# Grouped-query decode attention on one core: 8 MB tiles in three buffers, keys transposed in place, scores kept in PSUM

## The chip, the cores and the metric

The kernel runs on one core of a Trainium2 chip. The metric is device time in microseconds (us) of one execution. A core has TensorE (PE, matrix products; PEld is its weight load), VectorE (DVE), ScalarE (ACT), GpSimd (POOL) and SyncE (SP), each with its own queue of instructions, and 16 DMA engines. SP and ScalarE each have a queue of their own for the DMAs that they issue. SBUF is the on-chip memory of 128 partitions; PSUM is where TensorE writes.

## The reference

One query token attends to 65536 keys; 32 query heads share 8 heads of keys and values (4 query heads for each group), with head size 128, all in bf16.

```python
B, Hq, Hkv, Sq, Sk, D = 1, 32, 8, 1, 65536, 128
rep = Hq // Hkv
k = jnp.repeat(k, rep, axis=1)
v = jnp.repeat(v, rep, axis=1)
scores = jnp.einsum("bhqd,bhkd->bhqk", q, k) * D ** -0.5
p = softmax(scores, axis=-1)
out = jnp.einsum("bhqk,bhkd->bhqd", p, v)
```

Keys and values are 134 MB each, and every byte is needed once.

## The kernel before

The 65536 keys of a group lie as 512 rows on each of 128 partitions. A group's keys come as four tiles `kn` of 128 rows a partition (32 KB a partition, 4 MB), its values as four tiles `vb` of the same shape. All of them pass through one pool, `iopool`, with four buffers, and SP issues every load (L121 for keys, L202 for values). A load waits on SP until its buffer is free, and all later loads wait behind it.

The outer loop runs over groups g = 0..8, the inner one over tiles s = 0..3. In each turn `k_step(g, s)` works on a key tile of group g and `v_stream(g - 1, s)` on a value tile of the group before, so loads alternate key, value, key, value after the first four key tiles. The order of loads on SP is that of the program; a scheduler merges the instructions of the compute engines.

`k_step`: VectorE transposes 32x32 blocks of the key tile as 32-bit words (L135), two of eight row groups `w` at a time, from `kn` into a tile `T` (pool `tpool`, three buffers). TensorE multiplies with weights `wq` that hold the four queries at shifted columns (L144): 32 matmuls of 512 columns for a tile, all summed in one PSUM tile `sc` of 128x512. ScalarE copies `sc` to SBUF, into `S_g` (L151). There are two weight tiles, `Wq[0]` and `Wq[1]`, which GpSimd fills in turn (`queries`, L109).

`softmax(g)`: VectorE takes the maximum of `S_g` over 2048 columns (L156), TensorE and VectorE spread it over partitions (L160 to L174), ScalarE takes the exp of all 2048 columns into `E_g` with row sums (L177), and VectorE transposes `E_g` into `ET` (`transpose_weights`, L190). `E_g` and `ET` have two buffers each.

`v_stream`: 32 matmuls for a tile (L213), with 32 columns of `ET` as weights and 512 columns of values:

```python
for c in range(rows // W):
    for x in range(2):
        j = 2 * x + c % 2
        nc.tensor.matmul(out=o_tiles[g][32 * j:32 * j + 32, :, :], ...)
```

So j, the group of 32 output rows, runs 0, 2, 1, 3. `pick(g)` keeps the wanted blocks of `psum_o` (L224, L230), `finish` sums them, divides by the row sums and stores. The last value tile comes in pieces of 64, 32, 16, 8, 4 and 4 rows, and `finish_last` works them off with a written-out order on TensorE (L290, L287, L280, L297) up to the last store (L305).

At the start ScalarE issues four small loads of the queries, `qn` (L70), while SP issues the first key tiles. VectorE transposes `qn` and fills `wq` from it before the first keys can be used.

Of the kernel before, what the change touches and what calls it, by code (L numbers as in the profile page):

```python
# [13 lines left out]
NT = 128  # L14
NW = 16
# [5 lines left out]
def kernel(  # L21
# [26 lines left out]
    W = NT // NW  # L48
    assert W * HPG == 32 and KT == 4
# [6 lines left out]
    iopool = ctx.enter_context(tc.tile_pool(name="iopool", bufs=4))  # L56
    tpool = ctx.enter_context(tc.tile_pool(name="tpool", bufs=3))
    spool = ctx.enter_context(tc.tile_pool(name="spool", bufs=2))
    epool = ctx.enter_context(tc.tile_pool(name="epool", bufs=2))
    opool = ctx.enter_context(tc.tile_pool(name="opool", bufs=2))  # L60
    stats = ctx.enter_context(tc.tile_pool(name="stats", bufs=2))
    psc = ctx.enter_context(tc.tile_pool(name="psc", bufs=3, space=bass.MemoryType.PSUM))
    psm = ctx.enter_context(tc.tile_pool(name="psm", bufs=1, space=bass.MemoryType.PSUM))
    psf = ctx.enter_context(tc.tile_pool(name="psf", bufs=1, space=bass.MemoryType.PSUM))
# [3 lines left out]
    qn = const.tile([P, D], bf16)  # L68
    for a in range(4):
        nc.scalar.dma_start(out=qn[32 * a:32 * a + 32, :], in_=q[0, :, 0, :])  # L70
# [3 lines left out]
    Wq = []  # L74
    for x in range(2):
        wq = const.tile([P, 4 * WX], bf16, name=f"wq{x}")
        nc.vector.memset(wq[:, :], 0.0)
        Wq.append(wq)
# [17 lines left out]
    lsum_all = const.tile([P, Hkv], fp32)  # L96
    o_all = const.tile([P, Hkv, D], fp32)

# [5 lines left out]
    def queries(g):  # L104
        eng = nc.vector if g == 0 else nc.gpsimd
        wv = Wq[g % 2][:, :].rearrange("p (b r x) -> p b r x", b=2, r=2)
        for a in range(4):
            qd = slice(32 * a, 32 * a + 32)
            eng.tensor_copy(  # L109
                out=wv[qd, :, :, 32 * a + 28:32 * a + 28 + HPG],  # L110
                in_=qv[qd, :, :, g * HPG:(g + 1) * HPG],
            )
# [3 lines left out]
    S_tiles, E_tiles, ET_tiles, o_tiles = {}, {}, {}, {}  # L116

    def k_load(g, s):
        kn = iopool.tile([P, NT, D], bf16, name="kn", tag="io", align_bytes=2048)
        src = k[0, g].rearrange("(p n) d -> p n d", p=P)  # L120
        nc.sync.dma_start(out=kn[:, :, :], in_=src[:, s * NT:(s + 1) * NT, :])  # L121
        return kn

    def k_step(g, s, kn):
        if s == 0:
            S_tiles[g] = spool.tile([P, KT, 4 * P], fp32, name="S_g")
        wq = Wq[g % 2]
        kv = kn[:, :, :].rearrange("p (c w) d -> p w c d", w=W)
        sc = psc.tile([P, 4 * P], fp32, name="sc")
        for w in range(W):  # L130
            if s == 0 and w == W // 2 and g > 0:
                transpose_weights(g - 1)
            if w % 2 == 0:
                T = tpool.tile([P, 2, NW, D], bf16, name="T")
                nc.vector.transpose(  # L135
                    out=T[:, :, :, :].bitcast(fp32),
                    in_=kv[:, w:w + 2].bitcast(fp32),
                )
            Tv = T[:, w % 2].rearrange("p n (b i r) -> p n b i r", b=2, r=2)
            for b in range(2):  # L140
                for r in range(2):
                    bp = 2 * b + r
                    at = bp * WX + 28 - 4 * w
                    nc.tensor.matmul(  # L144
                        out=sc[:, :],
                        lhsT=wq[:, at:at + P],
                        rhs=Tv[:, :, b, :, r],
                        start=(w == 0 and bp == 0),
                        stop=(w == W - 1 and bp == 3),
                    )  # L150
        nc.scalar.copy(out=S_tiles[g][:, s, :], in_=sc[:, :])  # L151

    def softmax(g):
        S_g = S_tiles[g]
        mx = stats.tile([P, 1], fp32, name="mx")
        nc.vector.tensor_reduce(  # L156
            out=mx[:, :], in_=S_g[:, :, :].rearrange("p n c -> p (n c)"), axis=AX.X, op=ALU.max
        )
# [6 lines left out]
        mrow = stats.tile([1, P], fp32, name="mrow")  # L165
# [10 lines left out]
        E_g = epool.tile([P, KT, 4 * P], bf16, name="E_g")  # L176
        nc.scalar.activation(  # L177
            out=E_g[:, :, :].rearrange("p s x -> p (s x)"),
            in_=S_g[:, :, :].rearrange("p s x -> p (s x)"),
            func=ACT.Exp,  # L180
            bias=nmb[:, 0:1],
            scale=SCALE,
            accum_out=lsum_all[:, g:g + 1],
        )
        E_tiles[g] = E_g

    def transpose_weights(g):

        ET = epool.tile([P, KT, NW, 32], bf16, name="ET")
        nc.vector.transpose(  # L190
            out=ET[:, :, :, :].rearrange("p s c x -> p (s c x)"),
            in_=E_tiles[g][:, :, :].rearrange("p s x -> p (s x)"),
        )
        ET_tiles[g] = ET

    def v_load(g, s, pieces=(NT,)):
        vb = iopool.tile([P, NT, D], bf16, name="vb", tag="io", align_bytes=2048)
        src = v[0, g].rearrange("(p n) d -> p n d", p=P)
        x = 0
        for step in pieces:  # L200
            n0 = s * NT + x
            nc.sync.dma_start(out=vb[:, x:x + step, :], in_=src[:, n0:n0 + step, :])  # L202
            x += step
        return vb

    def v_stream(g, s, vb, rows, last):

        if s == 0:
            o_tiles[g] = pso.tile([P, 4, D], fp32, name="psum_o")
        for c in range(rows // W):  # L210
            for x in range(2):
                j = 2 * x + c % 2
                nc.tensor.matmul(  # L213
                    out=o_tiles[g][32 * j:32 * j + 32, :, :],
                    lhsT=ET_tiles[g][:, s, c, :],
                    rhs=vb[:, c * W + 4 * x:c * W + 4 * x + 4, :],
                    start=(s == 0 and c < 2),
                    stop=(last and c >= rows // W - 2),
                )

    def pick(g):

        o_m = opool.tile([P, 4, D], fp32, name="o_m")
        nc.vector.tensor_tensor(  # L224
            out=o_m[:, :, :],
            in0=o_tiles[g][:, :, :],
            in1=mask[:, :].unsqueeze(2).broadcast_to([P, 4, D]),
            op=ALU.mult,
        )
        nc.vector.tensor_reduce(  # L230
            out=o_all[:, g, :], in_=o_m[:, :, :].rearrange("p x d -> p d x"), axis=AX.X, op=ALU.add
        )

    def sums(g0, n):

        psum_l = psm.tile([HPG, n], fp32, name="psum_l", tag="misc")
        nc.tensor.matmul(out=psum_l[:, :], lhsT=sel[:, :], rhs=lsum_all[:, g0:g0 + n], start=True, stop=True)  # L237
        rl = stats.tile([HPG, n], fp32, name="rl")
        nc.vector.reciprocal(out=rl[:, :], in_=psum_l[:, :])
        return rl  # L240

    def store(g0, n, psum_f, rl):
        o_out = stats.tile([HPG, n, D], bf16, name="o_out")
        nc.vector.tensor_tensor(  # L244
            out=o_out[:, :, :],
# [5 lines left out]
            out=out[0, :, 0, :].rearrange("(g h) d -> h g d", h=HPG)[:, g0:g0 + n, :], in_=o_out[:, :, :]  # L251
        )

    def finish(g0, n):
        rl = sums(g0, n)
        psum_f = psf.tile([HPG, n, D], fp32, name="psum_f", tag="fin")
        nc.tensor.matmul(  # L257
            out=psum_f[:, :, :], lhsT=sel[:, :], rhs=o_all[:, g0:g0 + n, :], start=True, stop=True
        )
        store(g0, n, psum_f, rl)  # L260

    def finish_last(g, s, vb):
# [6 lines left out]
        v_stream(g, s, vb, n1, True)  # L269
        pick(g)  # L270
        psum_oT = pso.tile([P, HPG], fp32, name="psum_oT", tag="psum_o")
        psum_f = psf.tile([HPG, 1, D], fp32, name="psum_f", tag="fin")

        def w4(n):
            c, w = divmod(n, W)
            return ET[:, s, c, HPG * w:HPG * w + HPG]

        def single(a, b):
            for n in range(a, b):
                nc.tensor.matmul(  # L280
                    out=psum_f[:, 0, :], lhsT=w4(n), rhs=vb[:, n, :], start=False, stop=(n == NT - 1)
                )

        with tc.manual_schedule(engines={mybir.EngineType.PE}):
            for n in range(n1, n2):
                if n == n1 + 32:
                    nc.tensor.matmul(  # L287
                        out=psum_f[:, 0, :], lhsT=sel[:, :], rhs=o_all[:, g, :], start=True, stop=False
                    )
                nc.tensor.matmul(  # L290
                    out=psum_oT[:, :], lhsT=vb[:, n, :], rhs=w4(n), start=(n == n1), stop=(n == n2 - 1)
# [4 lines left out]
            psum_t2 = psm.tile([HPG, D], fp32, name="psum_t2", tag="misc")  # L296
            nc.tensor.transpose(out=psum_t2[:, :], in_=oT[:, :], identity=ident[:, :])  # L297
            single(n3, NT)
        o_t = stats.tile([HPG, D], fp32, name="o_t")
        nc.vector.tensor_scalar_mul(out=o_t[:, :], in0=psum_t2[:, :], scalar1=rl[:, 0:1])  # L300
        o_last = stats.tile([HPG, D], bf16, name="o_last")
        nc.vector.scalar_tensor_tensor(  # L302
            out=o_last[:, :], in0=psum_f[:, 0, :], scalar=rl[:, 0:1], in1=o_t[:, :], op0=ALU.mult, op1=ALU.add
        )
        nc.scalar.dma_start(out=out[0, g * HPG:(g + 1) * HPG, 0, :], in_=o_last[:, :])  # L305

    for g in range(Hkv + 1):
        if 0 < g < Hkv:
            queries(g)
        for s in range(KT):  # L310
            if g < Hkv:
                k_step(g, s, k_load(g, s))
            elif s == 0:
# [45 lines left out]
```

## Time and profile before

| | |
|---|---|
| median of 3 runs | 631.85 us (631.57 to 631.9) |
| profiled execution, its own time | 631.69 us |
| its span, first to last instruction | 629.6 us |
| granted TensorE clock, mean | 0.780 |
| TensorE busy | 363.2 us (58%), 2133 instructions |
| VectorE busy | 340.4 us (54%), 201 instructions |
| ScalarE busy | 36.8 us (6%) |
| GpSimd busy | 6.4 us (1%) |
| HBM read | 268.47 MB, 426 GB/s over the span |
| key transposes, L135 | 128 of 2277 ns |
| key matmuls, L144 | 1024, 445 ns |
| value matmuls, L213 | 1008, 403 ns |

Busy times are sums over the span, and the matmuls' means hold the time that they overlap each other. In the profile's slices the span is cut into 40 equal parts (15.7 us here); digits are tenths. A line of a timeline gives start, length, engine, line, operation, output and inputs, count, and in brackets the idle time before it and what ended that. Lines named Lnn are those of the kernel before.

### The profile page before, as it was taken

The numbers are of one execution on the slowest core, as the hardware profiler recorded it, in microseconds if no ns is written. First come the engines' busy times: TensorE is split into PE (matmuls) and PEld (weight loads), VectorE is DVE, ScalarE is ACT, GpSimd is POOL, SyncE is SP. The second block draws the span as 40 slices with busy tenths as digits, with TensorE's granted clock in tenths as the row PEclk, the third lists the DMA queues.
The fourth block names the chain that finished last, engine by engine and source line by source line (L and its number), as shares of the span: only waits on it lengthen the run. The fifth ranks groups of instructions, "written<-read, shape, count | busy, mean of one in ns | idle before, by whom it ended". The sixth has DMA issues, their size and how long they took to land.

```text
span 629.6 us, 4872 instructions
## 1 busy us (share of the span) xinstructions
PE 363.2 (58%) x2133; PEld 141.5 (22%) x2133; DVE 340.4 (54%) x201; ACT 36.8 (6%) x49; POOL 6.4 (1%) x37
## 2 busy tenths in 40 slices
PE   0686836745557554575645856447665466644645
PEld 0232312211222221222211222112221122211212
DVE  0998833774337753377543775436754366553511
ACT  0000100010000100001000010001000010000100
POOL 0000000000000000000000000000000000000000
PEclk9998988767887677876778867788677787767856
DMA  8999999999999999999999999999999999999996
GB/s 369 433 434 431 433 432 434 432 433 433 432 433 432 433 433 432 433 432 433 432 433 433 430 434 434 433 432 433 435 432 433 432 433 433 432 433 434 431 430 267
DMA packets 10192, 268.78 MB, mean 427 GB/s; under 512 B 1340, under 2 KB 1596, under 8 KB 1852
## 3 DMA queue, kind: packets, MB, share of 16 engines
q1 hardware_dynamic: 9936, 268.44, 99.0%
q8 instruction: 16, 0.26, 0.1%
q10 hardware_dynamic: 236, 0.04, 0.0%
q14 instruction: 4, 0.03, 0.0%
HBM read 268.47 MB, written 0.01 MB: 426 GB/s over the span
## 4 chain that ended last, share of the span: by engine, by line
DMA 73%; DVE 12%; issue 11%; PE 2%; ACTq 0%; DVEq 0%; SPq 0%
DMA kn<-in_k_dram 66%; DVE T L135 12%; DMA vb<-in_v_dram 5%; DMA qn<-in_q_dram 2%; PE sc L144 2%; PE psum_o L213 0%; PE psum_oT L290 0%; ACTq L70 0%; PE psum_f L280 0%; DVEq L135 0%; DVE wq L109 0%; PE psum_f L287 0%; DVE sel L83 0%; DVE o_last L302 0%; SPq L202 0%
## 5 line engine op out<-in xcount | busy, mean ns | idle before, releaser
L144 PE MATMUL sc<-T,wq 128*128 128x512 bf16 x1024 | 287.9, 445 | 220.2 <-DVE T L135 220.2
L135 DVE STREAM_TRANSPOSE T<-kn 128x2048 f32<-128x2048 f32 x128 | 284.2, 2277 | 198.6 <-DMA kn<-in_k_dram 198.6
L144 PEld LDWEIGHTS <-wq 128*128 128x128 bf16 x1024 | 109.5, 109 | 394.6 <-issue 159.5
L213 PE MATMUL psum_o<-vb,ET 128*32 128x512 bf16 x1008 | 65.1, 403 | 12.0 <-DMA vb<-in_v_dram 9.8
L151 ACT COPY S_g<-sc 128x512 f32<-128x512 f32 x32 | 18.8, 587 | 510.8 <-PE sc L144 510.8
L213 PEld LDWEIGHTS <-ET 128*32 128x32 bf16 x1008 | 25.5, 100 | 49.2 <-issue 28.3
L156 DVE TENSOR_REDUCE mx<-S_g 128x1 f32<-128x2048 f32 x8 | 18.3, 2286 | 26.1 <-ACT S_g L151 26.1
L190 DVE STREAM_TRANSPOSE ET<-E_g 128x2048 bf16<-128x2048 bf16 x8 | 18.5, 2311 | 16.3 <-ACT E_g L177 16.3
L177 ACT ACTIVATE E_g<-S_g,nmb 128x2048 bf16<-128x2048 f32 x8 | 16.0, 2001 | 47.6 <-DVE nmb L174 40.4
L224 DVE TENSOR_TENSOR o_m<-psum_o,mask 128x512 f32<-128x512 f32 x8 | 5.5, 682 | 21.5 <-PE psum_o L213 21.5
L109 POOL COPY wq<-qx 32x16 bf16<-32x16 bf16 x28 | 5.3, 190 | 426.9 <-PE sc L144 410.2
L160 PE MATMUL psum_t<-ident,mx 128*1 128x128 f32 x8 | 2.2, 270 | 11.2 <-DVE mx L156 11.2
L100 DVE STREAM_TRANSPOSE qx<-qn 128x64 f32<-128x64 f32 x1 | 0.2, 245 | 15.0 <-DMA qn<-in_q_dram 15.0
L172 PE MATMUL psum_b<-one,mrow 1*128 1x1 f32 x16 | 3.5, 288 | 8.3 <-DVE mrow L166 8.3
L230 DVE TENSOR_REDUCE o_all<-o_m 128x128 f32<-128x512 f32 x8 | 8.0, 1000 | 0.0
L172 PEld LDWEIGHTS psum_b<-one,mrow 1*128 1x128 f32 x16 | 3.0, 232 | 12.2 <-issue 11.4
L237 PE MATMUL psum_l<-lsum_all,sel 128*4 128x4 f32 (+2 forms) x6 | 0.6, 166 | 7.7 <-ACT E_g L177 7.7
L257 PE MATMUL psum_f<-o_all,sel 128*4 128x512 f32 (+1 forms) x4 | 2.6, 730 | 2.9 <-DVE o_all L230 2.9
L160 PEld LDWEIGHTS psum_t<-ident,mx 128*1 128x1 f32 x8 | 0.6, 79 | 15.1 <-DVE mx L156 11.6
L174 DVE COPY nmb<-psum_b 128x1 f32<-128x1 f32 x8 | 1.2, 152 | 2.9 <-PE psum_b L172 2.9
L290 PE MATMUL psum_oT<-ET,vb 128*128 128x4 bf16 x56 | 1.8, 167 | 1.4 <-DMA vb<-in_v_dram 1.4
L244 DVE TENSOR_TENSOR o_out<-psum_f,rl 4x512 bf16<-4x512 f32 (+1 forms) x2 | 1.2, 612 | 2.5 <-PE psum_f L257 2.5
(30 smaller groups left out, 16.1 us busy)
## 6 DMA issues: line engine op xcount, KB each, us to landing
kn<-in_k_dram SPq DMA_DIRECT2D x32, 4096.0 KB, 29.6
vb<-in_v_dram SPq DMA_DIRECT2D x31, 4096.0 KB, 34.1
vb<-in_v_dram SPq DMA_DIRECT2D x1, 2048.0 KB, 29.5
vb<-in_v_dram SPq DMA_DIRECT2D x1, 1024.0 KB, 31.6
vb<-in_v_dram SPq DMA_DIRECT2D x1, 512.0 KB, 32.3
vb<-in_v_dram SPq DMA_DIRECT2D x1, 256.0 KB, 32.5
vb<-in_v_dram SPq DMA_DIRECT2D x2, 128.0 KB
qn<-in_q_dram ACTq DMA_DIRECT2D x4, 8.0 KB, 10.1
```

The lines of the kernel that those rows point to most:

```text
L109: eng.tensor_copy(out=wv[qd, :, :, 32 * a + 28:32 * a + 28 + HPG], in_=qv[qd, :, :, g * HPG:(g + 1) * HPG],)
L135: nc.vector.transpose(out=T[:, :, :, :].bitcast(fp32), in_=kv[:, w:w + 2].bitcast(fp32),)
L144: nc.tensor.matmul(out=sc[:, :], lhsT=wq[:, at:at + P], rhs=Tv[:, :, b, :, r], start=(w == 0 and bp == 0), stop=(w == W - 1 and bp == 3),)
L151: nc.scalar.copy(out=S_tiles[g][:, s, :], in_=sc[:, :])
L156: nc.vector.tensor_reduce(out=mx[:, :], in_=S_g[:, :, :].rearrange("p n c -> p (n c)"), axis=AX.X, op=ALU.max)
L160: nc.tensor.transpose(out=psum_t[:, :], in_=mx[:, :], identity=ident[:, :])
L172: nc.tensor.matmul(out=psum_b[:, :], lhsT=mrow[:, :], rhs=one[:, :], start=True, stop=True)
L177: nc.scalar.activation(out=E_g[:, :, :].rearrange("p s x -> p (s x)"), in_=S_g[:, :, :].rearrange("p s x -> p (s x)"), func=ACT.Exp, bias= ...
L190: nc.vector.transpose(out=ET[:, :, :, :].rearrange("p s c x -> p (s c x)"), in_=E_tiles[g][:, :, :].rearrange("p s x -> p (s x)"),)
L213: nc.tensor.matmul(out=o_tiles[g][32 * j:32 * j + 32, :, :], lhsT=ET_tiles[g][:, s, c, :], rhs=vb[:, c * W + 4 * x:c * W + 4 * x + 4, :], ...
L224: nc.vector.tensor_tensor(out=o_m[:, :, :], in0=o_tiles[g][:, :, :], in1=mask[:, :].unsqueeze(2).broadcast_to([P, 4, D]), op=ALU.mult,)
L230: nc.vector.tensor_reduce(out=o_all[:, g, :], in_=o_m[:, :, :].rearrange("p x d -> p d x"), axis=AX.X, op=ALU.add)
```

## The change

- A tile is 256 rows a partition, 64 KB a partition, 8 MB, in three buffers (192 KB of SBUF a partition, for 128 KB). A group has two key tiles and two value tiles. A tile is worked off in two units of 128 rows.
- Keys are transposed in place, in four transposes of 64 rows (128x4096 words) a tile. `T` and its pool are gone. The row groups are contiguous rows now, no longer rows taken at a stride.
- `S_g` and its copies are gone. A unit's scores stay in PSUM tiles `sc` (five buffers), VectorE takes a maximum of each unit, and four exps of 512 columns read PSUM directly.
- One weight tile `wq`, one buffer each of `E_g` and `ET`; `E_g` is transposed right behind the exps in the program.
- `v_stream` runs over x outside and c inside, so j runs 0, 1, 0, 1, ... and then 2, 3, 2, 3, ...; its moving operand is four runs of 128 columns at a stride.
- `pick` is four instructions that read PSUM; `finish` runs for two groups at a time.
- The queries come in one load that repeats them four times. It and the loads of the first three tiles (group 0's two key tiles in four and two pieces, and group 1's first key tile) are issued by ScalarE, in that order and without a wait. SP issues all later loads, first group 0's first value tile, which takes the first buffer.
- The last value tile has a piece of 128 rows ahead of the pieces of before.

```diff
-NT = 128
+NT = 256
+NB = 128
-    iopool = ctx.enter_context(tc.tile_pool(name="iopool", bufs=4))
-    tpool = ctx.enter_context(tc.tile_pool(name="tpool", bufs=3))
-    spool = ctx.enter_context(tc.tile_pool(name="spool", bufs=2))
-    epool = ctx.enter_context(tc.tile_pool(name="epool", bufs=2))
+    iopool = ctx.enter_context(tc.tile_pool(name="iopool", bufs=3))
+    epool = ctx.enter_context(tc.tile_pool(name="epool", bufs=1))
-    psc = ctx.enter_context(tc.tile_pool(name="psc", bufs=3, space=bass.MemoryType.PSUM))
+    psc = ctx.enter_context(tc.tile_pool(name="psc", bufs=5, space=bass.MemoryType.PSUM))
...
-    for a in range(4):
-        nc.scalar.dma_start(out=qn[32 * a:32 * a + 32, :], in_=q[0, :, 0, :])
+    nc.scalar.dma_start(out=qn[:, :], in_=q[0, :, 0, :].unsqueeze(0).broadcast_to([4, Hq, D]))
...
+    def load(x, name, g, s, pieces=(NT,), eng=nc.sync):
+        t = iopool.tile([P, NT, D], bf16, name=name, tag="io", align_bytes=2048)
+        src = x[0, g].rearrange("(p n) d -> p n d", p=P)
+        n = 0
+        for step in pieces:
+            n0 = s * NT + n
+            eng.dma_start(out=t[:, n:n + step, :], in_=src[:, n0:n0 + step, :])
+            n += step
+        return t
...
+        for u in range(U):
+            nu = s * U + u
+            sc = psc.tile([P, 4 * P], fp32, name="sc")
+            sc_tiles[g, nu] = sc
+            for w in range(W):
+                n0 = u * NB + w * NW
+                if w % 4 == 0:
+                    groups = kn[:, n0:n0 + 4 * NW, :].rearrange("p n d -> p (n d)").bitcast(fp32)
+                    nc.vector.transpose(out=groups, in_=groups)
+                kv = kn[:, n0:n0 + NW, :].rearrange("p n (b i r) -> p n b i r", b=2, r=2)
...
-        nc.scalar.copy(out=S_tiles[g][:, s, :], in_=sc[:, :])
+            nc.vector.tensor_reduce(out=mx_tiles[g][:, nu:nu + 1], in_=sc[:, :], axis=AX.X, op=ALU.max)
...
+        for nu in range(NU):
+            nc.scalar.activation(
+                out=E_g[:, nu, :],
+                in_=sc_tiles[g, nu][:, :],
+                func=ACT.Exp,
...
-        for c in range(rows // W):
-            for x in range(2):
-                j = 2 * x + c % 2
+            for x in range(n):
+                for c in range(NW):
+                    j = 2 * x + c % 2
...
-                        rhs=vb[:, c * W + 4 * x:c * W + 4 * x + 4, :],
+                        rhs=vv[:, 4 * x:4 * x + 4, c, :],
...
+    first = {
+        (0, 0): load(k, "kn", 0, 0, pieces=(64, 64, 64, 64), eng=nc.scalar),
+        (0, 1): load(k, "kn", 0, 1, pieces=(NB, NB), eng=nc.scalar),
+        (1, 0): load(k, "kn", 1, 0, eng=nc.scalar),
+    }
...
-                    finish_last(g - 1, s, v_load(g - 1, s, pieces=(64, 32, 16, 8, 4, 4)))
+                    finish_last(g - 1, s, load(v, "vb", g - 1, s, pieces=(128, 64, 32, 16, 8, 4, 4)))
```

## The prediction

> **What bounds the kernel now.** I read the slices first, then the table of DMA queues, the chain, and the stretches around one key tile and around the end.
>
> ```profile
> DMA  8999999999999999999999999999999999999996
> GB/s 369 433 434 431 433 432 434 432 433 433 432 433 432 433 433 432 433 432 433 432 433 433 430 434 434 433 432 433 435 432 433 432 433 433 432 433 434 431 430 267
> q1 hardware_dynamic: 9936, 268.44, 99.0%
> q10 hardware_dynamic: 236, 0.04, 0.0%
> ```
>
> The transfers never pause: 38 slices stand at 430 to 435 GB/s, and only the first and last are lower. So the time is bytes over rate, plus a start and a tail. The bytes stay. What counts is whether the queue ever runs dry, and the rate.
>
> ```profile
> 81.16 29.74 DMA kn<-in_k_dram
> 111.19 2.07 issue
> 113.39 2.06 issue
> 115.45 4.47 DVE T L135 x2
> 119.94 29.87 DMA kn<-in_k_dram
> ```
>
> The chain (start, length, what) goes from a key load to VectorE's transposes of it, and from the last of these to the issue of a later load. The landings that VectorE waits for run from 72.25 to 577.43 us, 52 tiles apart: 9.715 us for 4 MB, so 19.4 us for an 8 MB tile.
>
> ```profile
> 94.07 8.47 PE L144 MATMUL sc<-T,wq 128*128 128x512 bf16 x32 [9.14 <-DVE T L135]
> 102.47 1.91 PE L213 MATMUL psum_o<-vb,ET 128*32 128x512 bf16 x32
> 111.02 8.89 DVE L135 STREAM_TRANSPOSE T<-kn 128x2048 f32<-128x2048 f32 x4 [10.44 <-DMA kn<-in_k_dram]
> 606.34 3.60 PE L213 MATMUL psum_o<-vb,ET 128*32 128x512 bf16 x32 [2.30 <-DMA vb<-in_v_dram]
> 616.01 3.38 PE L213 MATMUL psum_o<-vb,ET 128*32 128x512 bf16 x32 [6.06 <-DMA vb<-in_v_dram]
> 620.85 1.05 PE L213 MATMUL psum_o<-vb,ET 128*32 128x512 bf16 x16 [1.46 <-DMA vb<-in_v_dram]
> 627.31 0.27 ACTq L305 DMA_DIRECT2D out_dram<-o_last  x1
> ```
>
> The compute engines idle about half of the time: VectorE sits 10.44 us before a key tile. The last line shows that a small store, issue to landing, costs about 2 us (627.31 to the span's end at 629.6); I split that into 1.1 us from issue to first data (the slices allow about that at the start) and 1.0 us from last data to the waiting engine.
>
> ```profile
> L70 ACTq DMA_DIRECT2D qn<-in_q_dram x4: 418/438/650, 0.7 to 2.1; - x4
> DMA to landing us min/median/max: 5.9/10.1/14.3
> ```
>
> This is the decisive row. The four query loads are 8 KB each, on ScalarE's queue, beside key tiles on SP's. The packet counts fit one packet per partition row and a closing one per load and DMA engine (8832 + 69 x 16 = 9936), so the four loads give each engine 12 packets. A 32 KB packet lasts 9.7 / 8 = 1.21 us; 12 of them are 14.5 us, and the last query load took 14.3. So the two queues take turns, one packet each, and neither goes first.
>
> **Rate, start and tail.** Packets grow from 32 KB to 64 KB. Near the end the tile in 32 KB packets took 616.01 - 606.34 = 9.67 us and the next half tile, in 16 KB packets, 4.84: twice that is 9.68. Packet size is worth 0.1%, so I take -0.2 us (bounds -0.6 and 0). The Trainium skill, DMA: Bandwidth & Descriptors, section "Anatomy of one DMA — SWDGE (gpsimd) path", fits about 2 us of fixed cost to every transfer, and by it 69 loads becoming 42 would save 54 us; the two rows above speak against using it for queued loads.
>
> At the start, ScalarE issues one query load (0.44 us a load in that row) ahead of the first keys: +0.4. That load is now 128 rows from one instruction in place of four of 32; its packets cost between nothing and 0.5 us (the first slice lacks 64 / 433 x 15.7 = 2.3 us, of which issue to data is 1.1 and the wait before the issue 0.7, so 0.5 is the whole rest): +0.4, near the upper end. The Trainium skill, same page, "Rules for kernel authors", says that an outermost dimension of four copies confines a load to four DMA engines; no row of before shows such a load beside key tiles, and by that rule each of four engines would get 32 small packets, some 2 us late.
>
> At the tail the last value tile ends in the same shrinking pieces as before. Value matmuls are reordered: before, four in a row wrote four different 32-row groups, 0.06 us each (1.91 / 32); now two groups alternate. Between 0.06 (order is nothing) and 0.238 (no overlap, as L144's 1.90 / 8) I take 0.12. Then the 16 matmuls after the 64-row piece take 1.9 us for 1.05, where 1.4 us are free before the next piece: +0.5 (0 to +1.5).
>
> **Steady state: hidden.** A key tile needs 4 transposes of 4.4 us (two of L135's, 8.89 / 4 each), 17.6 us, and 16 matmuls after the last, 3.8: with landing and maxima it is free about 24 us after it landed. With three buffers, one being read and two queued, the queue lasts 2 x 19.4 = 38.8 us from a landing, less 1.1 to restart: 13.7 us to spare. A value tile lands 19.4 us after its key tile, waits for the keys' matmuls until 24, takes 64 x 0.12 = 7.7, and is free some 12 us after landing. The removed copies to S_g (0.59 each) and the second wq cost nothing either way: ScalarE is 6% busy, and keys of two groups lie 19.4 us apart, with 0.93 us of GpSimd copies between. Scores in PSUM are held until the exp; a fifth sc buffer covers the next group's first 128 rows. One ET buffer makes the transpose of E_g wait for the last value matmuls of the group before, and the next keys' transposes queue behind it on VectorE: about 13 us after that value tile, before the next key tile's 19.4. If that cover goes, it first eats the 13.7.
>
> **The first three tiles: the term that decides.** They are K00, K01, K10 (group, tile) on ScalarE's queue, 58.2 us of transfer with no wait. SP's first load, V00, takes K00's buffer. K00's four pieces land every 4.85 us from 2.7 + 4.85; the last, at 23.1, is transposed (4.4) and multiplied (3.8): V00 is issued at 31.6, its data run from 32.7. Before, all tiles came in one queue, in order. Now V00 takes turns with K01 and K10, which come first in need.
> - K01 ends between 50 (equal packets) and 59 (its 32 KB packets against 64 KB ones), instead of 41.5. Its second half is used up 14.6 us later (1.0 + 8.8 + 3.8 + 1), at 65 to 74. Then SP issues K11, again beside K10.
> - K10, 19.4 us of data, shares nearly throughout, and ends at 86 to 89 instead of 60.9: I take 87.
> - What is queued in all, five tiles, drains at 2.7 + 97 = 99.7 in any order. The next load, V01, needs K10's buffer, and everything behind it in SP's queue waits too.
> - K10 is free at 87 + 1.0 + 17.6 + 2.3 (ET of group 0 stands between its transposes in VectorE's order) + 0.6 (a maximum, L156's 2286 ns for a quarter of the columns) + 3.8 + 1.8 (24 value matmuls stand before its last 16) = 114.1. V01's data start at 115.2.
>
> So the DMA engines idle 115.2 - 99.7 = 15.5 us, once. Bounds: 12.3 (K10 at 86, landing in 0.5, value matmuls at no cost) to 22 (K10 at 89, value matmuls of 0.238, a first quarter of keys at 0.43 each, the pace L213 and L144 show after idling). Nothing gives it back, for nothing else bounds the kernel. After it no second gap follows: V01 lands at about 135, K11's buffer is free by 137, with K20 in transfer until 155.
>
> The Trainium skill, same page, "Queues, rings and completion order", says that an engine drains a whole packet of typically 9 to 17 descriptors from one queue before it switches. By that, whole tiles would alternate, K01 would finish before V00, K10 would land at 80, and the idle time would be 8 to 10 us; but the query loads would then have waited for whole tiles, 9.7 us each, and they did not.
>
> **Sum**, against the profiled execution: span 629.6 + 0.4 + 0.4 - 0.2 + 0.5 + 15.5 = 646.2. It took 631.69 with 2.1 us outside the span, 0.16 below the median of 631.85: 648.3 us. This case alone runs from 644 (631.7 + 12.3, other terms at their least) to 656.1 (631.7 + 22 + 0.4 + 0.5 + 1.5).
>
> **Rivals.**
> - No idle time, the forecast's opposite: the engines finish what ScalarE queued first, or V00 comes so late that it meets little of it. Then K10 lands at 62, is free before 90, V00's and K11's data are queued until 99.7, and the sum is 631.7 + 1.1 = 632.8, or 631.5 with the small terms at their least: no change. It decides from K10 landing before 72 or so (72 + 27.1 + 1.1 is the 99.7). For it: nothing else in before shows two large streams at once. Against it: the query row.
> - Idle time that comes back with every pair: TensorE at the slow pace throughout. Keys 64 x 0.427 + values 64 x 0.24 = 42.7 us for 38.8 of transfer; from 38.8 on each us costs 14 or so: 648 + 14 x 3.9 = 703, and 662 with one us over. Against it: the 8.47 us row is at full pace after its first five us, and a longer run per tile warms it better.
> - Something quicker than any row here, such as 64 KB packets 0.5% faster with no idle time: 629.
>
> **How the numbers follow.** One gap at the start 78%; no gap 12% (half within 0.2%, 1.3 us, about what a measurement can tell; the rest slower or faster); repeated gaps 7%; something quicker 3%. Leaving out the no-gap and quicker cases and the far end of the repeated ones is about 2 in 10: 643 to 657. Faster 0.08 (quicker, some of no gap, and a little for doubt in my reading of the queues), same 0.07, slower 0.85.
>
> **What would show it.** Right: one or two slices near 100 to 115 us far below 430 GB/s, and none later; VectorE idle from about 74 until K10 lands at 87; SP waiting for TensorE before V01; value matmuls near 0.12 us. Wrong: slices full throughout (then the queues do not take turns), or low slices again and again (then TensorE is short).

## The result and the profile after

The changed kernel takes 648.25 us (median of 5, 647.66 to 650.55); the kernel before, measured beside it, 631.9 us. The ratio is 1.0263, with a 95% interval of 1.0244 to 1.0283. The forecast was 648.3 us in a range of 643 to 657. The profiled execution took 647.66 us, of which 645.9 are the span, 16.3 more than before.

The slices and the two large queues of the changed kernel (a slice is 16.1 us here):

```profile
DMA  8999991799999999999999999999999999999996
GB/s 343 438 445 461 394 451 70 325 456 451 406 439 447 423 434 442 431 426 435 442 423 430 451 419 430 443 426 434 440 434 435 430 431 434 439 426 435 435 409 279
q1 hardware_dynamic: 5040, 243.27, 87.2%
q10 hardware_dynamic: 1192, 25.21, 9.2%
```

Slices seven and eight hold 70 and 325 GB/s; no later one falls below 400 until the tail. ScalarE's queue (q10) now moves 25 MB, the three early tiles. Weighed against the mean of the middle slices (433 GB/s), the first ten slices lack 18.4 us of transfer, where before they lacked 2.3: 16.1 us, nearly all of the 16.3.

Stretches of the span (busy time of PE, PEld, DVE, ACT and POOL, then granted clock, DMA share, GB/s):

```profile
95.00:100.00 5.00, 5.00 (x13) 1.74 (x12) 5.00 (x2) 0.00 (x0) 0.00 (x0) 0.50 0.97 419
100.00:105.00 5.00, 5.00 (x28) 1.96 (x26) 5.00 (x2) 0.00 (x0) 0.00 (x0) 1.00 0.00 0
105.00:110.00 5.00, 5.00 (x29) 1.80 (x28) 4.78 (x3) 0.00 (x0) 0.00 (x0) 1.00 0.00 0
110.00:115.00 5.00, 5.00 (x40) 2.19 (x40) 0.78 (x1) 0.00 (x0) 0.00 (x0) 1.00 0.01 3
115.00:120.00 5.00, 2.54 (x28) 0.86 (x25) 4.49 (x2) 0.00 (x0) 0.00 (x0) 1.00 1.07 406
```

For over 15 us no key or value moves while TensorE and VectorE are at work: here the kernel is bound by its engines, not by its transfers. These rates count a packet where it starts. By the start and length of each packet in the trace, the 16 DMA engines finish their last queued packets at 100.7 us on average and start on V01 at 116.7, 16.1 us later; their first packets then take 3.1 us each, for 2.42 later on. So about 16.7 us are lost.

SP's issues, VectorE's transposes and TensorE's last work on K10 in the changed kernel (start, length, what; in brackets the idle time before):

```profile
31.91 0.38 SPq L119 DMA_DIRECT2D vb<-in_v_dram  x1
...
73.94 0.33 SPq L119 DMA_DIRECT2D kn<-in_k_dram  x1
...
115.51 0.33 SPq L119 DMA_DIRECT2D vb<-in_v_dram  x1
```

```profile
59.93 4.45 DVE L134 STREAM_TRANSPOSE kn<-kn 128x4096 f32<-128x4096 f32 x1 [17.77 <-DMA kn<-in_k_dram]
...
90.23 4.45 DVE L134 STREAM_TRANSPOSE kn<-kn 128x4096 f32<-128x4096 f32 x1 [13.65 <-DMA kn<-in_k_dram]
94.59 2.27 DVE L180 STREAM_TRANSPOSE ET<-E_g 128x2048 bf16<-128x2048 bf16 x1
96.79 8.73 DVE L134 STREAM_TRANSPOSE kn<-kn 128x4096 f32<-128x4096 f32 x2
...
106.34 4.43 DVE L134 STREAM_TRANSPOSE kn<-kn 128x4096 f32<-128x4096 f32 x1
```

```profile
109.96 1.92 PE L196 MATMUL psum_o<-vb,ET 128*32 128x512 bf16 x24
111.82 3.66 PE L140 MATMUL sc<-kn,wq 128*128 128x512 bf16 x16
```

The three issues are V00, K11 and V01. VectorE waits 17.77 us for K01's second half and 13.65 us for K10, although these loads were issued before 6 us. K10, first used at 90.23, is followed by its transposes with ET between them; its last 16 matmuls end at about 115.5, and V01 goes out at 115.51.

### The profile page after: what moved, and what is told of

Read it like the earlier page. It is cut to its first block, busy times and chain, and to the rows that moved or that the text cites. A ratio compares the mean times of both kernels' runs of the same rounds, so it can differ in the third digit from the quotient of the medians.

```text
span 645.9 us, 4760 instructions
## 1 busy us (share of the span) xinstructions
PE 355.7 (55%) x2141; PEld 147.6 (23%) x2141; DVE 339.7 (53%) x193; ACT 23.6 (4%) x65; POOL 6.5 (1%) x37
## 4 chain that ended last, share of the span: by engine, by line
PE 27%; DVE 26%; DMA 23%; another core or an unknown queue 21%; ACT 1%; issue 1%; ACTq 0%; POOL 0%; SPq 0%; DVEq 0%
DVE kn L134 22%; PE sc L140 21%; DMA kn<-in_k_dram 18%; PE psum_o L196 5%; DMA vb<-in_v_dram 5%; ACT E_g L171 1%; DVE ET L180 1%; DVE o_pair L214 1%; DVE mx L147 1%; PE psum_b L165 0%; PE psum_f L233 0%; ACTq L119 0%; DVE o_pair L212 0%; DVE m L155 0%
## 5 line engine op out<-in xcount | busy, mean ns | idle before, releaser
L140 PE MATMUL sc<-kn,wq 128*128 128x512 bf16 x1024 | 266.9, 423 | 252.9 <-DVE kn L134 252.6
L134 DVE STREAM_TRANSPOSE kn<-kn 128x4096 f32<-128x4096 f32 x64 | 279.5, 4417 | 171.5 <-DMA kn<-in_k_dram 171.5
L140 PEld LDWEIGHTS <-wq 128*128 128x128 bf16 x1024 | 106.4, 105 | 411.1 <-issue 206.8
L196 PE MATMUL psum_o<-vb,ET 128*32 128x512 bf16 x1008 | 79.1, 399 | 10.0 <-DMA vb<-in_v_dram 10.0
L147 DVE TENSOR_REDUCE mx<-sc 128x1 f32<-128x512 f32 x32 | 21.6, 674 | 56.0 <-PE sc L140 56.0
L196 PEld LDWEIGHTS <-ET 128*32 128x32 bf16 x1008 | 35.0, 100 | 51.2 <-issue 20.3
L171 ACT ACTIVATE E_g<-sc,nmb 128x512 bf16<-128x512 f32 x32 | 21.6, 686 | 588.2 <-DVE nmb L167 588.2
L212 DVE TENSOR_SCALAR o_pair<-psum_o,mask 128x128 f32<-128x128 f32 x8 | 2.8, 351 | 48.9 <-PE psum_o L196 48.9
L180 DVE STREAM_TRANSPOSE ET<-E_g 128x2048 bf16<-128x2048 bf16 x8 | 18.4, 2303 | 11.7 <-ACT E_g L171 11.7
L214 DVE SCALAR_TENSOR_TENSOR o_pair<-psum_o,mask,o_pair 128x128 f32<-128x128 f32 x24 | 8.3, 346 | 0.5
L171 ACT ACTIVATION_READ_ACCUMULATOR E_g<-sc,nmb 128x1 f32 x32 | 6.5, 203 | 0.0
(31 smaller groups left out, 15.9 us busy)
## 6 DMA issues: line engine op xcount, KB each, us to landing
kn<-in_k_dram ACTq DMA_DIRECT2D x2, 4096.0 KB, 42.5
```

The source lines that it names most:

```text
L134: nc.vector.transpose(out=groups, in_=groups)
L140: nc.tensor.matmul(out=sc[:, :], lhsT=wq[:, at:at + P], rhs=kv[:, :, b, :, r], start=(w == 0 and bp == 0), stop=(w == W - 1 and bp == 3),)
L147: nc.vector.tensor_reduce(out=mx_tiles[g][:, nu:nu + 1], in_=sc[:, :], axis=AX.X, op=ALU.max)
L171: nc.scalar.activation(out=E_g[:, nu, :], in_=sc_tiles[g, nu][:, :], func=ACT.Exp, bias=nmb[:, 0:1], scale=SCALE, accum_out=lsum_all[:, g, ...
L180: nc.vector.transpose(out=ET[:, :, :, :].rearrange("p s c x -> p (s c x)"), in_=E_g[:, :, :].rearrange("p s x -> p (s x)"),)
L196: nc.tensor.matmul(out=o_tiles[g][32 * j:32 * j + 32, :, :], lhsT=ET_tiles[g][:, s * U + u, c, :], rhs=vv[:, 4 * x:4 * x + 4, c, :], start ...
```

## The experiments

All ratios are to the kernel before, run beside them on the same chip.

**E1, one queue.** The three early tiles are issued by SP.

```diff
-        (0, 0): load(k, "kn", 0, 0, pieces=(64, 64, 64, 64), eng=nc.scalar),
-        (0, 1): load(k, "kn", 0, 1, pieces=(NB, NB), eng=nc.scalar),
-        (1, 0): load(k, "kn", 1, 0, eng=nc.scalar),
+        (0, 0): load(k, "kn", 0, 0, pieces=(64, 64, 64, 64), eng=nc.sync),
+        (0, 1): load(k, "kn", 0, 1, pieces=(NB, NB), eng=nc.sync),
+        (1, 0): load(k, "kn", 1, 0, eng=nc.sync),
```

> The changed kernel with its first three tiles issued by SP instead of ScalarE, all loads in one queue; nothing else is changed. Theory (two queues take turns, so group 1's first key tile K10 lands late): K10 lands at about 60 us, is free by about 97, V01's load is queued before the queue drains at 99, no idle slice: 631 to 633 us. Rival (8 MB tiles in three buffers are too coarse for the start whoever issues): the gap of some 16 us stays, 645 to 649 us. Rival (value order, single weight tile or packets of 64 KB cost something in the steady state): between the two, 635 to 642 us, with no empty slice.

632.82 us, ratio 1.0016 (1.0007 to 1.0025). The large gap is gone, and with it 15 of the 16 us. The slices; then, of the timeline, VectorE's first use of the queries and SP's issue of V01:

```profile
GB/s 365 433 464 398 461 406 329 460 412 452 428 432 448 424 444 420 440 423 441 423 441 435 428 444 427 445 431 431 429 440 420 444 424 440 432 431 448 424 418 273
```

```profile
24.77 0.25 DVE L95 STREAM_TRANSPOSE qx<-qn 128x64 f32<-128x64 f32 x1 [23.56 <-DMA qn<-in_q_dram]
...
101.97 0.33 SPq L119 DMA_DIRECT2D vb<-in_v_dram  x1
```

The time was as expected, not every step: one slice has 329 GB/s, because K10 was free at 102 and not by 97. The queries came at 24.8 us, for now their load takes turns with key packets. E5 looks at this.

**E2, small packets on SP.** The issuing engines are as in the change; V00 and K11 come in four loads each, with packets of 16 KB for 64. Of each changed line only the call is shown.

```diff
-load(k, "kn", g, s)
+load(k, "kn", g, s, pieces=(64,) * 4 if (g, s) == (1, 1) else (NT,))
-load(v, "vb", g - 1, s)
+load(v, "vb", g - 1, s, pieces=(64,) * 4 if (g, s) == (1, 0) else (NT,))
```

> The changed kernel with only SP's first two loads, V00 and K11, cut into four pieces of 64 rows each (16 KB packets); ScalarE's loads stay as they are (K10 in 64 KB packets). Theory (turns of one packet each, whatever its size): ScalarE's queue then moves 64 KB for each 16 KB of SP's, K10 lands at about 66 instead of 89 us, its buffer is free at about 92, before the queue drains at 100: no gap, 632 to 634 us. Rival (the queues share by bytes): K10 lands as late as before, 645 to 649 us.

632.19 us, ratio 1.0001 (0.9991 to 1.0010): no gap. The slices; then VectorE's first transpose of K10:

```profile
GB/s 336 432 476 404 419 433 436 458 409 454 414 450 429 434 437 426 450 417 451 421 447 425 443 433 433 434 429 434 430 437 434 429 439 425 447 417 450 414 426 272
```

```profile
72.25 4.45 DVE L134 STREAM_TRANSPOSE kn<-kn 128x4096 f32<-128x4096 f32 x1 [7.94 <-DMA kn<-in_k_dram]
```

K10 is there at 72.25 instead of 90.23, with the same bytes queued on both sides. The expected 66 was too early; packets of half this size would give about 65. With 64 KB of K10 to 16 KB of SP's, 19.4 x 1.25 = 24.3 us after K01's end at about 46 (its second half is used from 48.25 on), it is 70 to 72. That sharing goes by packets and not by bytes follows from this run and the next together. Nor do whole loads take turns: then K01's second half would have been through ahead of V00, at about 42.5 us (2.7 + 38.8 + 1.0), and it was used at 48.25 here and at 59.93 in the change.

**E3, K10 in pieces.** The reverse of E2.

```diff
-        (1, 0): load(k, "kn", 1, 0, eng=nc.scalar),
+        (1, 0): load(k, "kn", 1, 0, pieces=(64, 64, 64, 64), eng=nc.scalar),
```

> The changed kernel with K10, still on ScalarE's queue, cut into four pieces of 64 rows (16 KB packets), so that its transposes can start on the first piece. Theory (turns of one packet each): K10 now gets 16 KB for each 64 KB of SP's queue and its last piece lands at about 100 us, when everything else has landed; its early pieces are used in the meantime, and its buffer is free at about 110 to 113: a gap of 11 to 15 us, 643 to 648 us. Rival (sharing by bytes): last piece at about 88, free at about 98, gap 0 to 2 us, 632 to 635 us.

645.62 us, ratio 1.0215 (1.0201 to 1.0229). Of the timeline, VectorE's transpose of K10's last piece and SP's issue of V01; then the slices:

```profile
102.32 4.45 DVE L134 STREAM_TRANSPOSE kn<-kn 128x4096 f32<-128x4096 f32 x1 [15.52 <-DMA kn<-in_k_dram]
...
111.90 0.33 SPq L119 DMA_DIRECT2D vb<-in_v_dram  x1
```

```profile
GB/s 343 441 447 405 449 452 72 453 396 456 448 401 452 441 411 449 440 415 437 448 421 432 441 432 428 441 432 428 445 428 433 440 425 440 433 428 440 429 410 243
```

Pieces, which let the transposes of K00 begin early, bring back only 2.6 of the 16 us here: the last piece is there 12 us later than whole K10 was, since each of its 16 KB packets waits for a 64 KB packet of K11.

**E4, the old tiles with the new issue.** The kernel before, with its first four key tiles issued by ScalarE.

```diff
-    def k_load(g, s):
+    def k_load(g, s, eng=nc.sync):
...
-        nc.sync.dma_start(out=kn[:, :, :], in_=src[:, s * NT:(s + 1) * NT, :])
+        eng.dma_start(out=kn[:, :, :], in_=src[:, s * NT:(s + 1) * NT, :])
...
+    first = {(0, s): k_load(0, s, nc.scalar) for s in range(KT)}
...
-                k_step(g, s, k_load(g, s))
+                k_step(g, s, first[g, s] if (g, s) in first else k_load(g, s))
```

> The kernel before with one change: its first four key tiles (4 MB each, four buffers) are issued by ScalarE behind the queries, all others by SP. Theory: the queues take turns here too, so the fourth tile K03 lands at about 60 us instead of 42, but it is worked off in 10 us instead of 27, its buffer is free at about 70 and the queue drains at about 71: a gap of 0 to 2 us, 631.5 to 635 us. Rival (two queues cost what they cost at any tile size): 645 to 649 us.

638.05 us, ratio 1.0092 (1.0078 to 1.0106): a miss by 3 us at the upper end, and well below the rival. The slices; then, of the timeline, two late value tiles on TensorE:

```profile
GB/s 332 429 429 428 420 373 434 436 429 431 430 433 436 433 437 432 431 430 431 434 433 441 432 429 428 431 431 436 437 434 435 428 431 431 436 435 434 433 422 225
```

```profile
611.33 2.57 PE L213 MATMUL psum_o<-vb,ET 128*32 128x512 bf16 x32 [2.68 <-DMA vb<-in_v_dram]
622.54 3.60 PE L213 MATMUL psum_o<-vb,ET 128*32 128x512 bf16 x32 [8.64 <-DMA vb<-in_v_dram]
```

The profiled span is 636.1, 6.5 us over the one before. Slices five and six lack (12 + 59) / 432 x 15.9 = 2.6 us: V01 was issued at 71.0, as expected, but K12 went out only at 82.2, when V01's data were about through, a step that the expectation had not followed. The first slice lacks 1.4 us more than before: ScalarE issues the keys behind four query loads. And one value tile near the end came 11.2 us after the one ahead of it, for the usual 9.7. That accounts for 5.5 us; why the late tile was slow stays open. So the new issue costs 6 us with 4 MB tiles in four buffers, some 4 of which are traced to its start, and 16 with 8 MB tiles in three.

**E5, one queue and the old query loads.** E1 with the queries in four loads of 32 rows.

```diff
-    nc.scalar.dma_start(out=qn[:, :], in_=q[0, :, 0, :].unsqueeze(0).broadcast_to([4, Hq, D]))
+    for a in range(4):
+        nc.scalar.dma_start(out=qn[32 * a:32 * a + 32, :], in_=q[0, :, 0, :])
```

> The changed kernel with its first three tiles issued by SP, as in the first experiment, and the queries again in four loads of 32 rows, as before the change. Theory: the gap of some 4 us that the first experiment kept comes from the queries, whose one load ran on four DMA engines with 32 packets each taking turns with SP's 16 KB packets and landed at 24.8 us; in four loads they have 12 packets on each engine, land at about 10 us, keys are used as they land, K10's buffer is free by 90 us, no gap is left, and the first key data come at 1.8 instead of 2.8 us: 631.0 to 632.0 us. Rival (8 MB tiles keep a gap of their own): 632.5 us or more, with a slice near 100 us below 400 GB/s.

631.82 us, ratio 1.0003 (0.9987 to 1.0020). Of the page, the slices and ScalarE's queue; then, of the timeline, the queries' first use and SP's issue of V01:

```profile
GB/s 364 439 467 401 463 405 458 408 455 413 452 421 443 425 442 430 433 442 422 446 418 454 418 446 421 447 421 443 433 429 439 433 434 429 434 438 430 439 405 252
...
q10 hardware_dynamic: 244, 0.04, 0.0%
```

```profile
11.26 0.24 DVE L96 STREAM_TRANSPOSE qx<-qn 128x64 f32<-128x64 f32 x1 [10.05 <-DMA qn<-in_q_dram]
...
88.67 0.33 SPq L120 DMA_DIRECT2D vb<-in_v_dram  x1
```

The queries are there at 11.3, V01 is issued at 88.7, some ten us before the queue would drain, and no slice is empty. Of the whole change, less its issue of tiles and of queries, no gain and no loss is left that these runs can tell.

**E6, K10 back on SP.** One tile less on ScalarE's queue.

```diff
-        (1, 0): load(k, "kn", 1, 0, eng=nc.scalar),
+        (1, 0): load(k, "kn", 1, 0),
```

> The changed kernel with K10 alone, the third of the first three tiles, issued by SP, ahead of all its other loads; K00 and K01 stay on ScalarE's queue. Theory (turns of one packet each): K10 starts at once in 64 KB packets against K00's 16 KB ones and lands at about 27 us, long before it is wanted, while K00 lands at about 42 instead of 22 and K01 at about 78 instead of 59. V00 and K11 are issued late, and the engines run dry twice, near 80 and near 115 us, 20 to 26 us in all: 652 to 658 us, slower than the change itself. Rival (what costs is that too many tiles are on ScalarE's queue): one tile less there makes the gap smaller, 635 to 645 us.

648.84 us, ratio 1.0266 (1.0248 to 1.0283). The slices; three stretches of the span, in the form of those above; then, of the timeline, SP's issues of V00, K11 and V01, and VectorE's first use of K01's second half:

```profile
GB/s 377 427 433 441 401 130 389 382 398 454 446 411 443 439 430 430 439 442 415 438 443 422 442 431 430 439 430 442 427 434 435 426 439 438 419 450 430 423 419 248
```

```profile
80.00:85.00 5.00, 3.48 (x9) 1.22 (x9) 5.00 (x3) 0.00 (x0) 0.00 (x0) 0.50 0.00 0
85.00:90.00 5.00, 5.00 (x23) 2.09 (x22) 5.00 (x2) 0.00 (x0) 0.00 (x0) 0.93 0.00 0
...
110.00:115.00 5.00, 5.00 (x26) 2.05 (x25) 0.60 (x1) 0.00 (x0) 0.00 (x0) 1.00 0.00 0
```

```profile
50.96 0.33 SPq L119 DMA_DIRECT2D vb<-in_v_dram  x1
...
77.02 4.45 DVE L134 STREAM_TRANSPOSE kn<-kn 128x4096 f32<-128x4096 f32 x1 [16.27 <-DMA kn<-in_k_dram]
...
90.72 0.33 SPq L119 DMA_DIRECT2D kn<-in_k_dram  x1
...
115.06 0.33 SPq L119 DMA_DIRECT2D vb<-in_v_dram  x1
```

The rival falls: one tile less on ScalarE's queue is no milder, and the engines run dry twice, where the theory put it. The size was off, 3 us below the expected range: by the packets' times the two stretches are 11.5 and 4.3 us, some 16 in all, not 20 to 26. K11 was issued at 90.72 and V01 at 115.06, and VectorE did ET of group 0 behind K10's transposes here, not between them.

**E7, ET behind K10.** The change, with group 0's ET transposed after K10's last keys.

```diff
+        E_tiles[g] = E_g
+        if g > 0:
+            weights(g)
+
+    E_tiles = {}
+
+    def weights(g):
+        E_g = E_tiles[g]
         ET = epool.tile([P, NU, NW, 32], bf16, name="ET")
...
+            if g == 1 and s == 0:
+                weights(0)
             if g > 0:
                 last = s == KT - 1
```

> The changed kernel with group 0's weight transpose ET moved behind K10's transposes in the program, so that neither it nor the value matmuls that need it stand between K10's landing and its last key matmuls. Theory (the gap ends when K10's buffer is free): K10 still lands at about 89 us, and its buffer is free after four transposes (17.5 us) and 16 matmuls (3.7), at about 111.5 instead of 115.5 us: 4 us less, 643.5 to 645 us. Rival (the gap ends with something else, such as V00's buffer): no change, 647.5 to 649 us.

644.28 us (641.05 to 644.96), ratio 1.0183 (1.0160 to 1.0206): 4.0 us less than the change by the medians, as expected, and 2.8 less by the profiled spans. VectorE's transposes of K10 and SP's issue of V01:

```profile
90.14 17.42 DVE L134 STREAM_TRANSPOSE kn<-kn 128x4096 f32<-128x4096 f32 x4 [15.24 <-DMA kn<-in_k_dram]
...
111.29 0.33 SPq L119 DMA_DIRECT2D vb<-in_v_dram  x1
```

K10 comes as late as in the change, its buffer is free 4.2 us earlier, and the kernel ends 3 to 4 us earlier. So the release of K10's buffer ends the gap, and most of what is saved on the way to it shows in the time (in E3, 2.6 of 3.6 us).

## Why the prediction was right

The mechanism and its place were right. That the total fits to 0.1 us is luck: smaller misses cancel, and the sum names 0.16 us to the median that it does not add (with it, 648.5). By its own terms:

- **Gap: 15.5 forecast, about 16.7 measured.** V00 went out at 31.91 (31.6), K11 at 73.94 (65 to 74), V01 at 115.51 (114.1). K11's time is at the end for packets of unequal size, which E2 and E3 bear out. K10's last row was through at 87.39 by the packets' times, as forecast, but it was first used at 90.23, not 1.0 us later. The packet that closes a load had come on 15 DMA engines by 86.2; on the last it came at 89.80, behind one more 64 KB row of K11 (87.39 to 89.81). So this landing waited for one more turn of the other queue, which the sum did not hold; in E3, with the other queue drained, K10's last row was through at 101.96 and used at 102.32. From 90.23 on, VectorE took 20.5 us for transposes, ET and maximum, as in the sum, and the rest 4.7 for 5.6. The first 16 matmuls of K10 took 6.20 us, TensorE having idled 18 us at half its clock, but VectorE waited only 0.22 us for TensorE.
- **Value matmuls: 0.12 us forecast, 0.07 to 0.12 measured**, all with two row groups in turn and at full clock: 1.92 us for the 24 above (0.080), 3.91 for 58 in a row (0.067), 1.90 for 16 near the end (0.119). Why they differ stays open; with four groups in turn it was 0.06. The sum had 1.8 us for the 24, for which 0.12 gives 2.9; of the measured 1.92, 1.05 came behind the last transpose.
- **Start: +0.8 forecast, 1.2 measured.** The query load of 128 rows took ScalarE 1.15 us to issue, one with 32 rows 0.44, so the first keys are issued at 1.92 for 0.74. I had taken the price of an issue from the smaller load.
- **Tail: +0.5 forecast, -0.5 measured.** The landing of the 32-row piece is seen at 623.31 of 629.6 before and 640.13 of 645.9 after, 6.3 and 5.8 us from the end. The 16 matmuls did take 1.90 us, but there was room for them; what came behind them was a little faster, at a granted clock of 1.00 from 640 to 642 us, for 0.50 from 624 on before.
- **Rate: -0.2 forecast, -1.3 measured.** From 157.98 to 584.58, 22 tiles of 8 MB came at 19.39 us, 9.695 for 4 MB against 9.715. Over 64 such tiles that is 1.3 us; the reference holds one load that came 1 us late, so little of it can be laid to the packets, and E5, which has these packets and no gap, was not measurably faster than before. Nothing like the 54 us that the prediction names for a fixed cost of each transfer shows.

Summed, 16.7 + 1.2 - 0.5 - 1.3 = 16.1, against 16.3 in the spans.

The steady state was hidden as argued: after the gap no slice is short, with one wq, one ET and three buffers, and E5 shows it for the whole kernel. The rival without a gap fell with the prediction's decisive row: two large queues share as the small query loads had shown, packet by packet. The Trainium skill, DMA: Bandwidth & Descriptors, section "Queues, rings and completion order", has an engine drain a packet of typically 9 to 17 descriptors before it switches queues; by whole tiles in turn, K10 would have landed at 80. It was there at 90.2, and E2 and E3, in which the same bytes came in smaller rows and more loads, moved it to 72 and its last piece to 102. Here each partition row counted as a packet of its own: by the packets' times of the changed kernel, each of the 63 rows of V00 (64 KB, 2.42 us) that start between 40 and 54 us starts within 0.03 us of the end of a row of K01 (32 KB, 1.21 us).

## What to carry to other kernels

Loads on two queues take turns, so a second queue does not add speed (by the packets' times, 433 GB/s from 37 to 64 us of the change, with both at work, and 433 later with one) but reorders what lands: what is needed next can come after what is needed later. Before early loads go on another queue, work out when each lands if both queues always have a packet ready, and whether its buffer is then free before everything queued has drained. Large tiles in few buffers make this dearer, since one late tile holds a third of the buffers for as long as it takes to work it off.

## What the runs showed of the hardware

- The share of a queue follows its packet size. With 16 KB against 64 KB packets, K10's use moved by 18 us (72.25 against 90.23) with the same bytes in both queues. Cutting a load into pieces of fewer rows slowed it beside a queue with large packets (E3) and let the other queue go ahead (E2).
- The query load with a leading dimension of four copies ran on four DMA engines only, by its closing packets. ScalarE's queue held 244 packets in E5 and 184 in E1; with the same data and stores, the 60 fewer are 64 closing packets against 4. The Trainium skill, DMA: Bandwidth & Descriptors, section "Rules for kernel authors", says that such a load is confined to as many engines as copies; the runs agree. Alone ahead of the keys it cost little (it was used at 3.1 us), beside 16 KB packets in E1 it was used at 24.8, as 32 turns of 0.6 us from its first packet at 5.4 us would have it.
